# Block attention of the first two batches: pairs of heads on a block diagonal, ahead of the MLP

## The chip, the cores and the metric

The kernel runs on one core of one Trainium2 chip. The metric is device microseconds of one execution, the median of the runs. TensorE is called PE below, VectorE DVE, ScalarE ACT, GpSimd POOL; SP is the engine that issues the DMAs.

## What is computed

```python
scores = scale * np.matmul(q, k.transpose(0, 1, 3, 2))     # 8 batches, 8 heads, 576 tokens, 64 dims
scores = np.where(block_i >= block_j, scores, -1000000000.0)  # blocks of 64 tokens
scores = scores - np.max(scores, axis=-1, keepdims=True)
attn = np.exp(scores)
attn = attn / (np.sum(attn, axis=-1, keepdims=True) + 1e-09)
x = np.matmul(attn, v)                                     # heads side by side: (8, 576, 512)
u = x + (x.transpose(0, 2, 1) @ U @ V).transpose(0, 2, 1)
y = u + np.maximum(u @ w_ch1, 0.0) @ w_ch2                 # 512 -> 2048 -> 512
out = (sigmoid(causal_conv5(y, conv_w)) * (y @ w_val)) @ w_out
```

q, k and v are float32, the weights float64. A query of block i sees the keys of blocks 0 to i.

## The kernel before, in words

**Stages.** 64 heads (8 batches of 8) go through attention, the 4608 tokens through the MLP in nine groups of 512 (group 0, 1, ...), and then through the gate stage. A group of the MLP has 16 steps f. Step f computes one slice h of 128 hidden features (`emit_h1`, L833, 12 matmuls), and with a lag of one step its share of the four accumulators (`emit_o`, L885, 12 matmuls). All these products are split into a high and a low fp32r part, so each is three matmuls.

**Attention is a generator.** `attention()` yields after each piece of work. Ahead of the MLP a loop draws pieces until one yields True. After that `gap()` draws them between the matmuls of the MLP, four gaps in a step; `aim(g)` sets how many pieces a gap draws: 72 pieces over 60 gaps in group 0, 68 over 60 in the others. A group begins only when the batch that it needs is mixed; what is missing by then is drawn at once, with no MLP work between (`while g > 0 and not pace[2]`). PE runs in program order; the other engines' queues are ordered by the framework's scheduler.

**Two kinds of heads.** Heads 0 to 15 (`NQ`, two batches) work by queries. `emit_q_bank` (L404) multiplies 128 queries with their keys, with K zero outside its head's 64 rows (`kz`, the tiles za and zb). DVE writes the mask into the PSUM banks (L418 to L422), takes row maxima (L425) and scales them (L427 to L432); ACT takes the exponential out of PSUM (L440). `emit_q_turn` transposes the result on PE (L456) and ACT copies it back (L457). Heads 16 to 63 work by keys (`emit_s_piece`, L381): the two heads of a pair lie on rows 0 to 63 and 64 to 127 of the array, and DVE works out and subtracts the maxima (L474 to L512). For all heads `emit_pv` (L604) multiplies with V, whose tile `vstk` has 64 columns of ones beside the 64 of V, so that the row sums come out as rows 64 to 127; ACT copies values (L605) and sums (L606), and `emit_norm_a`, `emit_norm_b` turn the sums and scale the values (L614 to L617 and L623 on DVE, L624 on POOL). From head `FIRST_SPLIT` = 18 on, V and the exponentials are split into fp32r parts; before that they are plain fp32, which takes two matmul instructions per product.

**Order.** `tick(n)` does the scores of head n, the values of head e = n - 2 and the transposes of head e + 1. `mixing` does the products with U and V for a pair of heads (`mix_T` L664, L672; `mix_G` L680; `mix_H` L703), which gives the u tiles of the MLP. Ticks 0 to 11 run ahead of the MLP, tick 12 to half of tick 20 in group 0, up to half of tick 28 in group 1.

**Conversions.** w_ch1 and w_ch2 are converted from float64 in 32 pieces (`split_w1`, `split_w2`): a load of 512 KB into one of two `raw` buffers, ACT (L118), four DVE operations (L120, L122, L123, L141), ACT and POOL for the parts (L89, L95), and for w_ch2 a store to `w2_s`, from which `load_w2` (L821) fetches it. The loop ahead of the MLP starts one at piece C0 = 4 and at every C1 = 12 pieces after it, 7 in all; group 0 starts four at step 0 and two at each further step.

```python
    for i, done in enumerate(stream):
        if i == UVAT:
            setup_uv()
        if i >= C0 and (i - C0) % C1 == 0 and len(convs) > 2 * NF - CMAX:
            conv(1)
        if done:
            break
```

Of the kernel before, what the change touches and what calls it, by code (L numbers as in the profile page):

```python
# [17 lines left out]
P = 128  # L18
# [4 lines left out]
def attn_moe_gate_kernel(ctx: ExitStack, tc: tile.TileContext, q, k, v, U, V, w1, w2, wval, convw, wout, out):  # L23
# [21 lines left out]
    FIRST_SPLIT = 2 * H + 2  # L45
# [6 lines left out]
    C0 = 4  # L52
# [23 lines left out]
    NPART = 0  # L76
    PAT = (0,1)
    URG = True
    UVAT = 10
# [222 lines left out]
    def setup_att():  # L302
        for t in vstk:
            pool.memset(t[:, :, D:P], 1.0)
            pool.memset(t[0:D, NK - 1, :], 0.0)
        for a in range(2):
            for t in kz:
                pool.memset(t[own[1 - a], a, :], 0.0)
# [60 lines left out]
    def emit_s_piece(pn, i):  # L369
# [31 lines left out]
    eqs = {}
    qmax = {}

    def emit_q_bank(n, i):  # L404

        a = n % 2
        tq, z = qkt[n // 2]
        if i == 0:
            s0, s1 = (s_p.tile([P, w], F32, tag=f"s{h}", name=f"s{h}") for h, w in enumerate(sw))
            eqs[n] = {3: s0[:, 0:4 * P], 1: s0[:, 4 * P:6 * P], 0: s1[:, 0:P], 2: s1[:, P:4 * P], 4: rot("m" if a else "mb", 1)}  # L410
            t = tiny_p.tile([P, 2 * NTT + 2], F32, tag="rq", name="rq")
            qmax[n] = (t[:, 0:NTT + 1], t[:, NTT + 1:], psum["a"].tile([P, 512], F32, tag="a", name="pS"))
        r, nm, _ = qmax[n]
        ps = psum["a"].tile([P, 512], F32, tag="a", name="pS") if i else _
        for t, k0, k1, o in qbanks[i]:
            pe.matmul(ps[:, o:o + k1 - k0], tq[:, kslice(t)], z[:, a, k0:k1], start=True, stop=True)  # L416
        if i == 0:
            vec.memset(ps[0:D, 4 * P - D:4 * P], MASKED)  # L418
        elif i == 2:
            vec.memset(ps[0:D, 3 * P - D:3 * P], MASKED)  # L420
        elif i == 3:
            vec.memset(ps.rearrange("p (c w) -> p c w", w=D)[0:D, 1:6:4, :], MASKED)  # L422
        for t, k0, k1, o in qbanks[i]:
            c = t + (k0 > 0)
            vec.reduce_max(r[:, c:c + 1], ps[:, o:o + k1 - k0], axis=AX.X)  # L425
        if i == 0:
            x = vec.tensor_scalar(nm[:, 3:4], r[:, 3:4], -scale, None, op0=ALU.mult)  # L427
        elif i == 2:
            vec.tensor_tensor(r[:, 4:5], r[:, 4:5], r[:, 5:6], op=ALU.max)
            x = vec.tensor_scalar(nm[:, 2:5:2], r[:, 2:5:2], -scale, None, op0=ALU.mult)  # L430
        elif i == 3:
            x = vec.tensor_scalar(nm[:, 0:2], r[:, 0:2], -scale, None, op0=ALU.mult)  # L432
        if i == 1:
            eqs[n]["wait"] = ps
            return
        noted(1, x)
        noted(3, x)
        for t, k0, k1, o in qbanks[i] + (qbanks[1] if i == 2 else []):
            src = eqs[n]["wait"] if i == 2 and t == NTT - 1 and k0 == 0 else ps
            act.activation(eqs[n][t][:, k0:k1], src[:, o:o + k1 - k0], AF.Exp, bias=nm[:, t:t + 1], scale=scale)  # L440

    def emit_q_turn(n):

        eq = eqs.pop(n)
        for i, (half, c0, blocks) in enumerate(tbanks):
            if c0 == 0:
                e = e_p.tile([P, sw[half]], F32, tag=f"e{half}", name="e")
                est[n, half] = (e,)
            ps = ps_p.tile([P, 512], F32, tag="a", name="pE")
            o = c = D if i == 0 else 0  # L450
            todo = []
            for t, j in blocks:
                todo.append((t == NTT - 1, o if t < NTT - 1 else o - D, t, j))
                o += P if t < NTT - 1 else D
            for _, at, t, j in sorted(todo, key=lambda x: not x[0]):
                pe.transpose(ps[:, at:at + P], eq[t][:, kslice(j)], ident)  # L456
            act.copy(est[n, half][0][:, c0:c0 + o - c], ps[:, c:o])  # L457
# [80 lines left out]
    def emit_est(n):  # L538

        if not 0 <= n < NH:  # L540
            return
        if n < NQ:
            with tc.high_priority():
                emit_q_turn(n)
            return
# [169 lines left out]
    def tick(n, mixed, last=B * NP):  # L715
# [3 lines left out]
        new, old = n < NH, 0 <= e < NH  # L719

        load_v(e + 1)
        for i in range(4):
            if n < NQ:
                with tc.high_priority():
                    emit_q_bank(n, i)
            elif new and n % 2 == 0:
                emit_s_piece(n // 2, i)
            if i == (0 if n % 2 else 3) and new and n >= NQ:
# [3 lines left out]
        if new:  # L732
            if n >= NQ:
                emit_max_b(n)
# [3 lines left out]
        if new and n >= NQ:  # L738
# [7 lines left out]
        if new and n >= NQ:  # L746
# [26 lines left out]
    def attention():  # L773

        for n in range(H + DEPTH + MORE):
            yield from tick(n, 0, NP)
        k = 0
        for at in range(2 * (H + MORE), 4 * (NP - 1) + H0 + 1):
            while k < NPART and at - 2 * (H + MORE) >= PAT[k]:
                h1_part(k)  # L780
                k += 1
            yield from mixing(at, 0, NP)
        for n in range(H + DEPTH + MORE, NH + DEPTH + HPOS // 2):
            yield from tick(n, NP)
# [264 lines left out]
    def aim(g):  # L1049

        if not pace[2]:
            end = 4 * (2 * NP - 1) + HPOS
            count = 6 * (end // 2 - H - MORE + 1) - 2 * (end % 2 == 0)
# [109 lines left out]
```

## Time and profile before

| | us |
|---|---|
| three runs | 1476.24, 1476.52, 1479.33; median 1476.52 |
| span of the profiled execution | 1473.3 |
| ahead of the MLP (0 to the first h) | 128.5 |
| group 0 of the MLP | 180.1 |
| group 1 | 134.3 |
| groups 2 and 3 | 133.6, 133.1 |
| group 8, with no attention in it | 86.3 |

The span reaches from the first to the last instruction of the profiled execution. Stages are cut at the first h of each group (192 matmuls of L833 each). A busy PE in the profile includes the tail of each matmul, so that 85% busy may still hide small holes.

### The profile page before, as it was taken

Reading aid. Unit: us, or ns where it says so; the run is one execution under the profiler, and the core shown is the slowest. Engines: PE = TensorE matmul, PEld = TensorE weight load, DVE = VectorE, ACT = ScalarE, POOL = GpSimd, SP = SyncE. Lnnn points to the kernel's source line nnn. Section 1 sums busy time; section 2 is a strip of 40 time slices with the busy share of each in tenths; the row PEclk is TensorE's granted clock in tenths of the full one; section 3 lists DMA queues with packets and bytes.
Section 4 is the critical chain, followed back from the end, with each engine's and each line's share of the span. In section 5 each row is a group of like instructions: output and inputs, shape, how many; then the busy total and the mean of one; then the engine's idle time right before and its main releaser. Section 6 shows DMA issues by size and latency. Waiting matters only on the chain.

```text
span 1473.3 us, 20082 instructions
## 1 busy us (share of the span) xinstructions
PE 1426.3 (97%) x6706; PEld 1102.3 (75%) x6706; DVE 1054.8 (72%) x2224; ACT 718.5 (49%) x1529; POOL 297.8 (20%) x420
## 2 busy tenths in 40 slices
PE   6888899899999999999999999999999999999999
PEld 3656666677777777777777777777888888788887
DVE  7878877967786888777778878777224326399991
ACT  4676564555555546565555555555322221344332
POOL 2113332212121112112211211121122100343310
PEclk9999999999999999999999999999999999999999
DMA  6445764543343434333434433332255433223311
GB/s 123 104 106 154 217 210 130 152 110 96 84 102 110 95 96 111 96 86 82 124 82 111 114 83 96 96 95 70 86 159 167 147 128 123 92 72 101 109 56 65
DMA packets 246288, 163.56 MB, mean 111 GB/s; under 512 B 197669, under 2 KB 212261, under 8 KB 246186
## 3 DMA queue, kind: packets, MB, share of 16 engines
q1 hardware_dynamic: 246186, 162.29, 39.6%
q8 instruction: 53, 0.87, 0.3%
q14 instruction: 49, 0.40, 0.1%
HBM read 134.98 MB, written 27.26 MB: 110 GB/s over the span
## 4 chain that ended last, share of the span: by engine, by line
PE 82%; DVE 10%; DMA 3%; ACT 2%; issue 1%; SPq 1%; POOL 0%; DVEq 0%; ACTq 0%
PE acc L885 25%; PE h L833 25%; PE pPV L604 8%; PE o L999 7%; PE val L975 6%; PE pS L381 6%; DMA raw<-in_moe_w_ch_dram 1%; DVE wa L123 1%; DVE rq L425 1%; PE pG L680 1%; PE acc L878 1%; PE pS L416 1%; DVE wa L141 1%; PE pT L664 1%; DVE wa L120 1%
## 5 line engine op out<-in xcount | busy, mean ns | idle before, releaser
L885 PE MATMUL acc<-hh,w 128*128 128x512 f32 x1152 | 401.0, 402 | 0.0
L885 PEld LDWEIGHTS acc<-hh,w 128*128 128x128 f32 x1152 | 217.1, 188 | 67.6 <-issue 22.5
L833 PE MATMUL h<-uh,w1hi 128*128 128x512 f32 x576 | 238.5, 414 | 2.3 <-ACT lt L606 1.2
L833 PE MATMUL h<-uh,w1lo 128*128 128x512 f32 x576 | 226.4, 393 | 0.0
L885 PE MATMUL acc<-hl,w 128*128 128x512 f32 x576 | 225.9, 392 | 0.0
L833 PE MATMUL h<-ul,w1hi 128*128 128x512 f32 x576 | 225.7, 392 | 0.0
L862 DVE SCALAR_TENSOR_TENSOR hl<-h,hh 128x512 fp32r<-128x512 f32 x144 | 98.5, 684 | 143.2 <-ACT hh L861 142.0
L861 ACT ACTIVATE hh<-h 128x512 fp32r<-128x512 f32 x144 | 85.9, 596 | 173.9 <-PE h L833 167.9
L833 PEld LDWEIGHTS h<-uh,w1hi 128*128 128x128 f32 x576 | 108.6, 189 | 45.7 <-issue 20.4
L95 POOL TENSOR_TENSOR vlo<-vstk,vhi 128x320 fp32r<-128x320 f32 x46 | 43.0, 934 | 455.3 <-ACT vhi L89 389.2
L833 PEld LDWEIGHTS h<-uh,w1lo 128*128 128x128 f32 x576 | 108.4, 188 | 24.2
L885 PEld LDWEIGHTS acc<-hl,w 128*128 128x128 f32 x576 | 108.8, 189 | 19.8 <-issue 0.7
L833 PEld LDWEIGHTS h<-ul,w1hi 128*128 128x128 f32 x576 | 108.7, 189 | 19.6 <-issue 1.3
L957 DVE SCALAR_TENSOR_TENSOR gt<-yb,cw,gt 128x516 f32<-128x516 f32 (+1 forms) x144 | 115.2, 830 | 1.4
L381 PE MATMUL pS<-tq,tk 64*128 64x320 f32 (+4 forms) x576 | 96.7, 429 | 1.5 <-DVE hl L862 0.8
L95 POOL TENSOR_TENSOR yl<-yb,yh 128x512 fp32r<-128x512 f32 (+7 forms) x64 | 66.9, 1078 | 107.4 <-ACT yh L89 107.3
L386 ACT COPY s<-pS 128x320 f32<-128x320 f32 (+2 forms) x128 | 60.2, 497 | 48.7 <-PE pS L381 47.5
L95 POOL TENSOR_TENSOR ul<-xt,uh 128x512 fp32r<-128x512 f32 (+7 forms) x64 | 53.8, 850 | 108.0 <-ACT uh L89 107.9
L536 ACT ACTIVATE s<-s 128x448 f32<-128x448 f32 (+1 forms) x62 | 44.0, 710 | 64.8 <-DVE s L512 64.8
L381 PEld LDWEIGHTS pS<-tq,tk 64*128 64x128 f32 x576 | 43.8, 185 | 37.8 <-issue 22.2
L512 DVE TENSOR_TENSOR s<-s,mb 128x64 f32<-128x64 f32 (+4 forms) x160 | 68.7, 493 | 0.3
L605 ACT COPY xt<-pPV 64x128 f32<-64x128 f32 (+1 forms) x128 | 50.1, 391 | 25.8 <-PE pPV L604 23.9
(169 smaller groups left out, 2758.8 us busy)
## 6 DMA issues: line engine op xcount, KB each, us to landing
w<-w_s SPq DMA_DIRECT2D x144, 512.0 KB, 3.3
rawq<-in_q_dram SPq DMA_DIRECT2D x128, 72.0 KB, 2.8
rawk<-in_k_dram SPq DMA_DIRECT2D x128, 72.0 KB, 3.1
out_dram<-ot SPq DMA_DIRECT2D x35, 256.0 KB, 2.0
vstk<-in_v_dram SPq DMA_DIRECT2D x64, 128.0 KB, 2.7
raw<-in_moe_w_ch_dram SPq DMA_DIRECT2D x64, 128.0 KB, 2.8
raw<-in_moe_w_ch_dram SPq DMA_DIRECT2D x16, 512.0 KB, 3.9
w_s<-wo SPq DMA_DIRECT2D x16, 512.0 KB, 3.3
```

Source lines behind the costliest of these rows:

```text
L95: eng.tensor_tensor(o, i, f32(h), op=ALU.subtract)
L381: pe.matmul(t[:, o:o + w], tk[me, kslice(j)], tq[me, a0:a1], start=True, stop=True)
L386: act.copy(stt[n][half_of[j]][:, d:d + o], t[:, 0:o])
L512: noted(3, vec.tensor_tensor(sv(n, j), sv(n, j), mb[:, q0[j]:], op=ALU.subtract))
L604: pe.matmul(o_, l_, r_, start=(i == 0), stop=(i == len(todo) - 1))
L833: pe.matmul(ps[:, 0:n], w[:, d, fs], x[:, d, 0:n], start=(d == 0 and i == 0), stop=(d == ND - 1 and i == 2))
L861: act.activation(hh[:, 0:n], ps[:, 0:n], AF.Relu)
L862: latest[0] = vec.scalar_tensor_tensor(hl[:, 0:n], ps[:, 0:n], 0.0, f32(hh[:, 0:n]), op0=ALU.max, op1=ALU.subtract)
L885: pe.matmul(acc[d][:, 0:n], w[:, wi, ds], x[:, 0:n], start=False, stop=(f == NF - 1 and i == 2))
L957: vec.scalar_tensor_tensor(gt[d][:, 0:gw], y[:, d, j:j + gw], cw[:, d, j:j + 1], gt[d][:, 0:gw], op0=ALU.mult, op1=ALU.add)
L975: pe.matmul(ps[:, 0:n], w[:, d, es], x[:, d, 0:n], start=(i == 0), stop=(i == 3 * ND - 1))
L999: pe.matmul(ps[:m, cs], x[:, e, a:a + m], w[:, e, cs], start=(i == 0), stop=(i == 3 * ND - 1))
```

## The change

Heads 0 to 15 are taken by pairs and by blocks of 64 queries. Q of a pair goes on a block diagonal (`qdiag`: columns (block, head, query)), so that one matmul gives 64 queries of both heads against exactly the keys they may see; the mask goes. A pair is worked in two halves u, blocks 6 to 8 and blocks 0 to 5. ACT sums the exponentials as it computes them (`accum_out`), and the exponentials are divided before they are transposed: blocks 0 to 5 on DVE, 6 to 8 on POOL. The values of the two heads are two matmuls with 64 columns of V each, written side by side on partitions 0 to 63 and 64 to 127 of one bank. All 16 heads start ahead of the MLP (`slot(u)`, u = 0 to 15); slots 16 to 20 are drawn in group 0, 12 pieces, and ticks 16 and later begin in group 1. Conversions ahead of the MLP: pieces 10, 22, ..., 106, nine in all. Heads 16 and 17 are split like the later ones.

```diff
-    FIRST_SPLIT = 2 * H + 2
+    FIRST_SPLIT = 2 * H
-    C0 = 4
+    C0 = 10
+    BREAK = 2 * H - 1
+    ONVEC = (0, 1, 2, 3, 4, 5)
-    UVAT = 10
+    UVAT = 14
...
+    def vpart(n):
+        c = D if n < NQ and n // 2 % 2 else 0
+        return vstk[n % 2][:, :, c:c + D]
...
+    def qdiag(t):
+        return t.rearrange("p (i a q) -> p i a q", a=2, q=D)
...
+            for a in range(2):
+                vec.transpose(qdiag(z)[own[a], :, a, :], t["q"][own[a]].rearrange("p (i q) -> p i q", q=D))
...
+                vec.transpose(tk, t["k"])
...
+    qbanks = (
+        ([(8, 0, 4 * P, 0, 0)],
+         [(8, 4 * P, S, 0, 1), (6, 0, 7 * D, D, 2)],
+         [(7, 0, 8 * D, 0, 3)]),
+        ([(5, 0, 6 * D, 0, 0), (1, 0, 2 * D, 6 * D, 1)],
+         [(4, 0, 5 * D, 0, 2), (2, 0, 3 * D, 5 * D, 3)],
+         [(3, 0, 4 * D, 0, 4), (0, 0, D, 4 * D, 5)]),
+    )
+    tbanks = (
+        ([(0, 6, 9), (4, 8, 9)], [(1, 6, 9)], [(2, 6, 9)], [(3, 6, 9)]),
+        ([(0, 0, 4)], [(0, 4, 6), (2, 4, 6)], [(1, 2, 6)]),
+    )
...
+        for i, k0, k1, o, c in todo:
+            pe.matmul(ps[:, o:o + k1 - k0], z[:, i * P:(i + 1) * P], tk[:, k0:k1], start=True, stop=True)
+        for i, k0, k1, o, c in todo:
             vec.reduce_max(r[:, c:c + 1], ps[:, o:o + k1 - k0], axis=AX.X)
...
+            act.activation(eblk[i][:, k0:k1], src[:, o:o + k1 - k0], AF.Exp, bias=nm[:, c:c + 1], scale=scale, accum_out=l[:, c:c + 1])
+    def emit_q_norm(u):
...
+        vec.tensor_scalar(l[:, 0:n], l[:, 0:n], 1e-9, None, op0=ALU.add)
+        vec.reciprocal(rec[:, 0:n], l[:, 0:n])
...
+                    (vec if i in ONVEC else pool).tensor_scalar(eblk[i][:, 0:w], eblk[i][:, 0:w], rec[:, c:c + 1], None, op0=ALU.mult)
+    def emit_q_turn(u, b):
+        ps = (ps_p if b % 2 else psum["a"]).tile([P, 512], F32, tag="a", name="pE")
...
+                pe.transpose(ps[:, c:c + P], eblk[i][:, kslice(j)], ident)
...
+        act.copy(e, ps[:, 0:c])
+    def emit_q_pv(u, part):
...
+                for a in range(2):
+                    pe.matmul(
+                        ps[own[a], (a0 - i0) * D:(a1 - i0) * D].rearrange("p (i q) -> p i q", q=D),
+                        vpart(2 * pn + a)[:, j, :], ev[:, :, a, :],
...
+            act.copy(xt[:, i0 * D:i1 * D], turned.pop(u)[:, 0:(i1 - i0) * D])
+    def slot(u):
...
+    def attention():
+        for a in range(4):
+            load_v(a)
+        for u in range(NQ + 5):
+            for done in slot(u):
+                yield done
+            if u == BREAK:
+                yield True
+            if u == NQ + 1:
+                ones_v()
+        for n in range(NQ, NH + DEPTH + HPOS // 2):
+            yield from tick(n, 2 * NP)
...
-            count = 6 * (end // 2 - H - MORE + 1) - 2 * (end % 2 == 0)
...
+            count = 12
             pace[:] = [0.0, (count if g == 0 else 8 * H + NP) / (4.0 * NF - SPARE), 0]
```

`slot(u)` emits, in this order and each followed by a yield: bank 0 of half u; the first part of the values of half u - 2; bank 1; the second part of the values (after which, for odd u, V of the next pair is loaded); bank 2 and the division of half u (for odd u also `prep_t` of the next pair, with its loads of q and k); the transposes of half u - 1; and the mixing steps, H for u = 2 pair + 6, G at + 5, T at + 4.

## Rows read from the trace of the kernel before

**Rows 1.** The page: busy time, share of the span, instructions of each engine.

```profile
PE 1426.3 (97%) x6706; PEld 1102.3 (75%) x6706; DVE 1054.8 (72%) x2224; ACT 718.5 (49%) x1529; POOL 297.8 (20%) x420
```

**Rows 2.** Stages: us, then PE, weight loads, DVE, ACT, POOL busy, clock, DMA share.

```profile
0.00:128.50 128.50, 101.86 (x477) 67.90 (x477) 97.38 (x281) 80.77 (x194) 25.55 (x38) 0.97 0.50 114
128.50:308.60 180.10, 164.42 (x731) 118.36 (x732) 149.61 (x309) 99.22 (x211) 54.92 (x60) 0.97 0.59 172
308.60:442.90 134.30, 133.59 (x657) 102.61 (x657) 104.78 (x232) 73.53 (x156) 24.15 (x44) 1.00 0.38 98
...
1177.40:1263.70 86.30, 86.30 (x382) 71.51 (x381) 37.67 (x55) 16.95 (x29) 0.11 (x1) 1.00 0.38 122
```

**Rows 3.** PE's longest wait ahead of the MLP: us in total, times, longest.

```profile
PE pE L456 <- ACT lt L606: 7.9, 7, 2.3
```

**Rows 4.** Timeline of PE ahead of the MLP: start, us to the last end.

```profile
45.71 3.41 PE L416 MATMUL pS<-za,tq 128*128 128x512 f32 x12
...
50.51 2.98 PE L604 MATMUL pPV<-e,vstk 128*128 128x128 f32 x12
...
53.76 0.27 PE L456 MATMUL pE<-ident,m 128*128 128x128 f32 x1
53.87 0.49 PE L456 MATMUL pE<-ident,s 128*128 128x128 f32 x3
```

**Rows 5.** Timeline of PE in group 2: a pair's scores between matmuls of the MLP.

```profile
600.62 0.39 PE L833 MATMUL h<-uh,w1lo 128*128 128x512 f32 x1
600.94 0.81 PE L381 MATMUL pS<-tq,tk 64*128 64x320 f32 x4
601.67 0.50 PE L833 MATMUL h<-uh,w1hi 128*128 128x512 f32 x1
```

**Rows 6.** Groups of DVE from 7 to 128.5 us: busy us, mean ns, idle before.

```profile
L425 DVE TENSOR_REDUCE rq<-pS 128x1 f32<-128x512 f32 (+2 forms) x72 | 31.2, 469 | 0.7 <-PE pS L416 0.2
...
L614 DVE STREAM_TRANSPOSE t<-lt 128x576 f32<-128x576 f32 x5 | 3.9, 774 | 3.9 <-ACT lt L606 3.9
...
L705 DVE TENSOR_TENSOR xt<-pH,xt 128x512 f32<-128x512 f32 (+1 forms) x8 | 3.4, 436 | 0.2
L623 DVE STREAM_TRANSPOSE t<-r 128x576 f32<-128x576 f32 x4 | 3.1, 768 | 0.0
...
L422 DVE MEMSET pS<- 64x128 f32 x12 | 2.0, 165 | 1.0 <-PE pS L416 0.8
...
L430 DVE TENSOR_SCALAR rq<-rq 128x2 f32<-128x2 f32 x12 | 1.9, 156 | 0.0
```

**Rows 7.** Timelines: steps of one conversion on DVE, and POOL beside it.

```profile
145.89 0.42 DVE L120 TENSOR_SCALAR wa<-wa 128x512 f32<-128x512 f32 x1
...
146.81 1.71 DVE L123 SCALAR_TENSOR_TENSOR wa<-raw,wa 128x512 uint32<-128x512 uint32 x1
148.55 0.69 DVE L141 SCALAR_TENSOR_TENSOR wa<-raw,wa 128x512 uint32<-128x512 uint32 x1
...
146.70 1.27 POOL L95 TENSOR_TENSOR w1lo<-wa,w1hi 128x512 fp32r<-128x512 f32 x1 [2.01 <-ACT w1hi L89]
```

**Rows 8.** ACT ahead of the MLP: a copy (timeline), the exponentials (group).

```profile
51.24 0.27 ACT L605 COPY xt<-pPV 64x128 f32<-64x128 f32 x1
...
L440 ACT ACTIVATE s<-pS,rq 128x512 f32<-128x512 f32 (+3 forms) x46 | 23.0, 537 | 15.9 <-DVE rq L427 10.4 <-DVE rq L430 4.3 <-DVE rq L432 1.0
```

**Rows 9.** DMA issues from 128.5 to 275 us: count, KB, us to landing.

```profile
raw<-in_moe_w_ch_dram SPq DMA_DIRECT2D x12, 512.0 KB, 3.9
...
w<-w_s SPq DMA_DIRECT2D x11, 512.0 KB, 4.3
```

**Rows 10.** The last DVE step of each conversion (L141), first and last stretch.

```profile
128.50:150.00 21.50, 4.34 (x5) 1.00 0.61 181
...
255.00:280.00 25.00, 2.26 (x4) 1.00 0.73 200
```

**Rows 11.** PE's scores by keys (L381) in group 1.

```profile
308.60:442.90 134.30, 16.01 (x96) 7.30 (x96) 1.00 0.38 98
```

More of the change, by code (lines that the diff above doesn't have):

```diff
@@ new lines, in attn_moe_gate_kernel, with emit_q_bank @@
+    half_i = ((6, 9), (0, 6))
+    halves = {}
+    turned = {}
+    def emit_q_bank(u, b):
+        pn, g = divmod(u, 2)
+        z, tk = qkt[pn]
+        if b == 0:
+            t = tiny_p.tile([P, 24], F32, tag="rq", name="rq")
+            halves[u] = [t[:, 6 * c:6 * c + 6] for c in range(4)] + [None]
+        r, nm, l, _, wait = halves[u]
+        ps = psum["a"].tile([P, 512], F32, tag="a", name="pS")
+        todo = qbanks[g][b]
+        for i, k0, k1, o, c in todo:
+            pe.matmul(ps[:, o:o + k1 - k0], z[:, i * P:(i + 1) * P], tk[:, k0:k1], start=True, stop=True)
+        for i, k0, k1, o, c in todo:
+            vec.reduce_max(r[:, c:c + 1], ps[:, o:o + k1 - k0], axis=AX.X)
+        if g == 0 and b == 0:
+            halves[u][4] = ps
+            return
+        c0, c1 = todo[0][4], todo[-1][4] + 1
+        todo = [(ps, x) for x in todo]
+        if wait is not None:
+            vec.tensor_tensor(r[:, 0:1], r[:, 0:1], r[:, 1:2], op=ALU.max)
+            vec.tensor_copy(r[:, 1:2], r[:, 0:1])
+            c0 = 0
+            todo = [(wait, qbanks[0][0][0])] + todo
+            halves[u][4] = None
+        x = vec.tensor_scalar(nm[:, c0:c1], r[:, c0:c1], -scale, None, op0=ALU.mult)
@@ L436, in emit_q_bank @@
         noted(1, x)
         noted(3, x)
[L438 to L457, printed above, removed]
+        for src, (i, k0, k1, o, c) in todo:
+            act.activation(eblk[i][:, k0:k1], src[:, o:o + k1 - k0], AF.Exp, bias=nm[:, c:c + 1], scale=scale, accum_out=l[:, c:c + 1])
@@ new lines, in emit_q_pv @@
+    def emit_q_pv(u, part):
+        pn, g = divmod(u, 2)
+        if part == 0 and g == 0:
+            xts[pn] = x_p.tile([P, S], F32, tag="xt", name="xt")
+        xt = xts[pn]
+        i0, i1 = half_i[g]
+        if part == 0:
+            turned[u] = ps_p.tile([P, 512], F32, tag="a", name="pPV")
+        ps = turned[u]
+        n = len(tbanks[g])
+        for b in range(n)[(0, 2)[part]:(2, n)[part]]:
+            c = 0
+            e = turned.pop((u, b))
+            for k, (j, a0, a1) in enumerate(tbanks[g][b]):
+                w = (a1 - a0) * P
+                ev = e[:, c:c + w].rearrange("p (i a q) -> p i a q", a=2, q=D)
+                c += w
+                last_ = b == n - 1 and k == len(tbanks[g][b]) - 1
+                for a in range(2):
+                    pe.matmul(
+                        ps[own[a], (a0 - i0) * D:(a1 - i0) * D].rearrange("p (i q) -> p i q", q=D),
+                        vpart(2 * pn + a)[:, j, :],
+                        ev[:, :, a, :],
+                        start=b == 0 and k == 0,
+                        stop=last_,
+                    )
+        if part == 1:
+            act.copy(xt[:, i0 * D:i1 * D], turned.pop(u)[:, 0:(i1 - i0) * D])
+            last[0] = (own[0], xt[own[0]][0:1, i0 * D:i0 * D + 1])
@@ L538, in emit_est @@
     def emit_est(n):
[L540 to L544, printed above, removed]
+        if not NQ <= n < NH:
             return
@@ L732, in tick @@
         if new:
-            if n >= NQ:
-                emit_max_b(n)
+            emit_max_b(n)
             if n % 2 == 1:
@@ L737, in tick @@
         yield from mixing(2 * e, mixed, last)
-        if new and n >= NQ:
+        if new:
             for _ in emit_max_c(n):
@@ L745, in tick @@
             yield
-        if new and n >= NQ:
+        if new:
             emit_exp(n)
@@ L1051, in aim @@
         if not pace[2]:
-            end = 4 * (2 * NP - 1) + HPOS
-            count = 6 * (end // 2 - H - MORE + 1) - 2 * (end % 2 == 0)
-            for delay, steps in ((HPOS, 2), (GPOS, 1), (TPOS, 2)):
-                count += steps * sum(2 * H <= 4 * pn + delay <= end for pn in range(NP, 2 * NP))
+            count = 12
             pace[:] = [0.0, (count if g == 0 else 8 * H + NP) / (4.0 * NF - SPARE), 0]
```

178 lines of the change are left out of this document (103 added, 75 removed).

## The prediction

> **What bounds the kernel now.** I began with the page: PE is busy 97% of the span, the next engine 72% [rows 1], so time can only come from PE's work or from holes in it. An average over stages says little here, so the second view was the busy time by stage [rows 2]. The reader is to see three things. Ahead of the MLP, PE has 101.9 us of 128.5 and DVE 97.4: neither is full, they wait for each other. Group 0 takes 180.1 us, though a group without attention takes 86.3; DVE is at 149.6 there, with most of the conversions on it. In group 1 PE is full (133.6 of 134.3) and DVE is at 78%. From group 2 on the change touches nothing: the same ticks end at the same place. So the sum is over three stages, which end at 442.9 us today, and the 1030.4 us behind them stay. The third view was what PE waits for ahead of the MLP: most of all, 7.9 us, for the copies of the row sums (L606) [rows 3]. The fourth was the timeline, for what one piece costs PE [rows 4, 5].
>
> **PE's work.** One head's scores are 1856 columns in 3.41 us [rows 4]; without some 0.25 us by which a last matmul outlasts its turn, 1.70 ns a column. A pair takes 2 x 1856 columns now, then 64 x (1 + ... + 9) = 2880: 832 x 1.70 = 1.4 us less, 11 us over 8 pairs. Transposes go from 30 to 25 a pair at 0.11 us ((0.49 - 0.27) / 2, from three in a row and one alone [rows 4]): 40 x 0.11 = 4.4 us less. The values keep their columns, 3200 a pair, 2.73 us a head (2.98 less the tail [rows 4]). Their cost is open, since the trace shows no two matmuls side by side in columns of the array. The nearest row has two side by side in rows: four scores of 320 columns on 64 rows each end after 0.81 us [rows 5], where one after the other they would take 4 x 0.27 + 0.25 = 1.33. So at best the 43.7 us of 16 heads halve, 22 us less; at worst nothing is gained. Going in and out costs something in the same rows: L381 begins 0.32 us after a matmul of the MLP, whose turn is 0.23 (86.3 us for 382 [rows 2]), and the next one 0.73 after L381 instead of 0.54: 0.28 us a visit. The values are visited 32 times: 9 us. I take the halved time less the visits, 13 us. The Trainium skill (TensorEngine Tiling (Array Packing), Key Properties) says that a change of tiling mode, not of the tile alone, drains the engine, which speaks against many short visits; the 0.28 us agrees with it.
>
> **Ahead of the MLP.** Today this stage has 12 heads' scores and 10 heads' values, then 16 and 14. PE will need 8 x 2880 columns x 1.70 = 39 us, transposes of 15 halves 21, values of 14 heads 38 (19 + 8 with overlap), mixing some 9: 96 to 107 us, against 88 by the same prices today. DVE decides. By rows 6: maxima 80 instead of 72 in 1.03 times the columns, +2; transposes of q and k for two more pairs, at 0.77 each, +4; masks gone (2.0 in L422, as much in its two smaller siblings), -4; small steps (maxima scaled, sums added, reciprocals) 96 instead of 48 at 0.16, +8; division of blocks 0 to 5, 48 instructions of 224 columns in the mean, 0.27 each between 0.156 for two columns and 0.42 for 512 [rows 6, 7], +13; row sums no longer turned, -7 in L614 and L623, -1.5 in the steps between; mixing of one and a half pairs more (L705 has 3.4 us for four, its siblings as much), +2.6; two conversions more at 2.2 (two steps of 0.42, two of 0.69 [rows 7]), +4.5. That is +21.6. The divisions of blocks 6 to 8 go to POOL, 24 of 448 to 576 columns, nearest row 1.27 us for 512 [rows 7], and beside that row DVE's L123 took 1.71 instead of 0.69. Between nothing and 24 x 1.0 us falls on DVE; I take 5, since most of DVE's work in those moments is maxima, read from PSUM. The Trainium skill (GPSIMD Engine Reference, Specifications) says that POOL shares its SBUF interfaces with DVE and contends with some of DVE's forms; L123 agrees. If that held for each of the 24, the stage would be 19 us of DVE longer than with my 5.
>
> DVE thus goes from 97.4 to 124. Without 7 us of start, in which it has 2.3, it now works 95.1 of 121.5 us; the 7.9 us for L606 go with the sums [rows 3], which makes 84%. (124 - 2.3) / 0.84 + 7 = **152**. At 92% it would be 139, at today's 78% 163. ACT loses the eight copies of values and sums a pair for two. Its sums within the exponential have no row: between nothing and one small copy of 0.27 us [rows 8], for 88 of them 24 us; I take 0.1 each, and all of it is hidden as long as ACT is 81 of 128.5 us busy [rows 2]. The division lies between a half's last exponential and its transposes: some 6 us (maximum 0.5, exponential 0.5, four small steps, three on POOL at 1.3 [rows 6 to 8]), covered by the next half's banks and another's values, 5 to 7 us of PE; without that cover it is rival (c). SP issues the loads of q, k (16) and V (8) of four more heads in this stage; DMA is half idle there. The memsets of the ones move behind slot 17, to an idle POOL.
>
> **Group 0.** 86.3 us for the MLP and what is left of the pairs: transposes of half 15 (1.3), values of two halves (4), mixing of two to three pairs (5): 97. Conversions are 23 now, with less to hide them. A `raw` buffer goes round in 3.9 us of load [rows 9], 2.2 on DVE [rows 7] and about 1.7 for ACT and the hand-offs: 7.8 us with two buffers, 3.9 a conversion. The last w_ch1 piece is ready 22 x 3.9 + 3 = 89 us after the start and wanted at 15/16 of 97, 91; the last w_ch2 piece after 90 + 3 and a store and a load of about 4 each [rows 9], 101, and wanted at 99. SP issues in order, and the fetches of w_ch2 stand behind loads that wait for a buffer. I add 8: **105**, between 97 and 125.
>
> **Group 1.** It takes over three pairs of scores (16.0 / 4 = 4.0 us each [rows 11]) and two heads' values (2.7 each): 134.3 + 17.4 = 152. Ticks 16 to 28 are 92 pieces, and 62 gaps draw 62 x 68/60 = 70 of them. The other 22 run without the MLP: PE has 22/68 of 48 us (134.3 - 86.3), 15.5, DVE up to 22/68 of 104.8, 34 [rows 2]. Between 0 and 18 us of holes; I take 4, as DVE's part can mostly run on into group 2, where it has room: **156**. Heads 16 and 17 in split form cost much the same.
>
> **Sum.** 152 + 105 + 156 = 413 instead of 442.9, 29.9 us less: against the profiled execution's span of 1473.3 that is 1443.4. The median stands 3.2 us above that span; with them **1446.6**.
>
> **Rivals.** (a) *It goes better*: DVE at 92%, two values at a time, conversions keep up: 139 + 98 + 152 = 389, 54 less, 1422.6. For it: rows 5. Against: DVE has never been so full ahead of the MLP. 16%. The Trainium skill (TensorE: Matmul & The Clock Gate, Part 3) gives column tiles that run concurrently; no row here shows them. (b) *The values don't overlap*, so that one point of the change fails: PE has 107 + 9 = 116 us ahead of the MLP; at today's 88 of 121.5 that takes 160, from 7 us on 167; 428 in all, 15 less, 1461.6. Against it: rows 5. 12%. (c) *The chain bounds*: a half costs what a head costs today, 121.5 / 12 = 10.1 us, because maximum, exponential, sum, division and transposes follow one another; 7 + 162 = 169; 430 in all, 13 less, 1463.6. For it: both engines wait today. Against: the longest wait goes. 11%. (d) *Slower, because the conversions bound group 0.* Today 25 of them end between 128.5 and 280 us, 6.1 us each [rows 10]. At that pace 23 take 140, with store and load 148: 152 + 148 + 156 = 456, 13 more, 1489.6. It decides from 5.5 us a conversion ((442.9 - 152 - 156 - 8) / 23). For it: two buffers and SP's order stay. Against: DVE is rid of the attention that came between their steps. 13%.
>
> **How the numbers follow.** My forecast has 48%. Its own range is 1430 to 1462, from stages of 139 to 163, 97 to 115 and 152 to 160 that don't all end on one side. A measurement here can tell some 0.2%, 3 us, from no change. Faster: 48 + 16 + 12 and half of (c), 82%; same, edges of (c) and (d), 5%; slower 13%. The range reaches from 1420, inside (a), to 1478, short of (d).
>
> **What would show it.** The first h near 152 us, group 1's near 257, group 2's near 413. Right: matmuls of the values in twos, no wait of PE for sums, DVE some 84% busy ahead of the MLP, conversions 4 us apart in group 0. Wrong: values at 2.7 us a head (b), PE waiting for POOL ahead of the transposes (c), PE waiting for w1lo or w in group 0 (d), a long hole at the end of group 1.

## The result, and the profile after

The changed kernel took 1485.93 us, median of 5 runs (1485.39 to 1489.71), beside 1476.52 for the kernel before on the same chip: 1.0074 times as long, with a 95% interval of 1.0052 to 1.0097. Slower by 0.7%; 1446.6 had been predicted, in a range that ended at 1478. The profiled execution took 1485.87 us, with a span of 1484.0.

First the page, to be read beside [rows 1]: PE has 21 us less to do, ACT 16 less, DVE as much as before.

```profile
PE 1405.5 (95%) x6736; PEld 1087.3 (73%) x6736; DVE 1054.6 (71%) x2215; ACT 702.2 (47%) x1545; POOL 329.3 (22%) x442
```

Then the stages, cut at the first h of each group as in [rows 2], with the same columns. The last line is the stage ahead of the MLP without its first 7 us.

```profile
0.00:162.20 162.20, 113.03 (x670) 73.78 (x670) 122.36 (x346) 89.42 (x276) 63.77 (x64) 0.94 0.47 107
162.20:279.90 117.70, 105.28 (x470) 81.06 (x468) 86.03 (x128) 47.85 (x92) 38.90 (x33) 0.97 0.67 223
279.90:452.90 173.00, 160.84 (x761) 118.97 (x760) 143.81 (x332) 98.87 (x208) 32.09 (x65) 0.96 0.36 88
452.90:586.10 133.20, 133.20 (x658) 102.56 (x657) 106.28 (x240) 73.99 (x156) 24.17 (x45) 1.00 0.40 99
...
7.00:162.20 155.20, 113.03 (x670) 73.78 (x670) 120.31 (x344) 87.94 (x274) 59.49 (x45) 0.93 0.47 107
```

Nearly the whole difference lies in the three stages, as the prediction had it: they end at 452.9 instead of 442.9, and behind them are 1031.1 us instead of 1030.4. Two sums over them say what happened. PE's busy time fell from 399.9 us [rows 2] to 379.2 (113.0 + 105.3 + 160.8): the 21 us that the change takes from PE did go. Its idle time rose from 43.0 to 73.8, 31 us. DVE's work is the same (351.8 [rows 2], now 352.2) and lies elsewhere: 25 us more ahead of the MLP, 39 more in group 1, 64 less in group 0, where it is now idle for 32 us of 118. By stages, PE stands idle 22 us more ahead of the MLP and 11 more in group 1, and 3 less in group 0.

**Ahead of the MLP.** What PE waits for, in place of the row sums of [rows 3]: the division on POOL, then the exponentials. The 8.1 us are the start, the first loads and transposes.

```profile
PE pS L445 <- DVE tq L378: 8.1, 1, 8.1
...
PE pE L500 <- POOL s L479: 22.0, 13, 6.0
PE pE L500 <- ACT s L463: 7.7, 5, 3.2
```

The groups of this stage that answer to [rows 6 to 8] (busy us, mean ns, idle time before): maxima, divisions on DVE and on POOL, and a line that the source does not show, since each exponential with `accum_out` is followed by a separate read of the accumulator.

```profile
L447 DVE TENSOR_REDUCE rq<-pS 128x1 f32<-128x512 f32 (+4 forms) x80 | 33.0, 449 | 11.4 <-PE pS L445 11.0
L479 DVE TENSOR_SCALAR s<-s,rq 128x384 f32<-128x384 f32 (+5 forms) x48 | 18.5, 454 | 0.2
...
L479 POOL TENSOR_SCALAR s<-s,rq 128x576 f32<-128x576 f32 (+2 forms) x24 | 38.9, 1634 | 61.3 <-DVE rq L474 31.7 <-ACT t L503 24.7 <-ACT x L91 4.9
...
L463 ACT ACTIVATION_READ_ACCUMULATOR s<-pS,rq 128x1 f32 x80 | 16.5, 206 | 0.0
```

The timeline of one half's end (start, us, what; in brackets the idle time before) shows the chain in one piece: the last exponential, the read of its sum, the reciprocal, three divisions in a row of 1.74 us each, and PE, which has nothing else to do meanwhile. From 60.10 to the twelve transposes at 66.53 are 6.4 us, in which PE stood idle for 3.5 and 1.3.

```profile
59.58 0.64 ACT L463 ACTIVATE s<-pS,rq 128x448 f32<-128x448 f32 x1
...
60.10 0.21 ACT L463 ACTIVATION_READ_ACCUMULATOR s<-pS,rq 128x1 f32 x1
...
60.88 0.18 DVE L474 RECIPROCAL rq<-rq 128x4 f32<-128x4 f32 x1
...
61.26 5.21 POOL L479 TENSOR_SCALAR s<-s,rq 128x576 f32<-128x576 f32 x3 [2.48 <-DVE rq L474]
...
64.78 0.48 PE L500 MATMUL pE<-ident,s 128*128 128x128 f32 x1 [3.48 <-POOL s L479]
...
66.53 2.82 PE L500 MATMUL pE<-ident,s 128*128 128x128 f32 x12 [1.28 <-POOL s L479]
```

**Group 0.** PE's waits there are for `hl`, a step of the MLP on DVE, which stands in DVE's queue behind steps of the conversions; and ACT waits for the loads of the conversions.

```profile
PE acc L998 <- DVE hl L975: 8.1, 7, 2.2
PE acc L998 <- ACT hh L974: 2.1, 2, 1.4
...
ACT wa L120 <- DMA raw<-in_moe_w_ch_dram: 33.0, 18, 3.3
```

**Group 1.** PE is busy for 160.8 us of the 173.0 here, 27 us more than in [rows 2], and idle for 12.2. The scores (first line, L406) take 33.4 us where [rows 11] has 16.0, the values (second line, L719) 28.2.

```profile
279.90:452.90 173.00, 33.40 (x168) 15.97 (x168) 0.96 0.36 88
...
279.90:452.90 173.00, 28.23 (x150) 24.79 (x150) 0.96 0.36 88
```

The values of this stage in the kernel before (L604) took 21.4:

```profile
308.60:442.90 134.30, 21.36 (x120) 18.76 (x120) 1.00 0.38 98
```

The last h of the group ends at 412 us, and from 420 to 448 PE has no matmul of the MLP at all: attention and mixing are drawn alone, with waits for DVE and for ACT's copies of the scores.

```profile
PE pG L795 <- DVE x L97: 5.3, 2, 5.2
PE pS L406 <- ACT za L411: 2.7, 2, 2.1
```

In the last 23 us of the stage DVE is 97% busy (22.3 of 23), and PE's granted clock is 0.83 and 0.61 of full speed in the mean: after that wait of 5.2 us, part of the time passes at the lower of its two levels (1.2 instead of 2.4 GHz).

```profile
430.00:440.00 10.00, 6.91 (x36) 5.50 (x36) 9.65 (x26) 3.34 (x9) 1.78 (x2) 0.83 0.16 31
440.00:453.00 13.00, 10.37 (x23) 6.17 (x24) 12.68 (x30) 8.86 (x18) 3.25 (x8) 0.61 0.18 46
```

### The profile page after: what moved, and what is told of

Its sections match the earlier page's. It is cut to its first block, busy times and chain, and to the rows that moved or that the text cites. A ratio compares the mean times of both kernels' runs of the same rounds, so it can differ in the third digit from the quotient of the medians.

```text
span 1484.0 us, 20191 instructions
## 1 busy us (share of the span) xinstructions
PE 1405.5 (95%) x6736; PEld 1087.3 (73%) x6736; DVE 1054.6 (71%) x2215; ACT 702.2 (47%) x1545; POOL 329.3 (22%) x442
## 4 chain that ended last, share of the span: by engine, by line
PE 77%; DVE 8%; DMA 4%; ACT 2%; issue 1%; POOL 1%; SPq 0%; ACTq 0%; DVEq 0%; POOLq 0%
PE acc L998 24%; PE h L946 23%; PE pPV L719 7%; PE o L1112 7%; PE val L1088 6%; PE pS L406 5%; DMA raw<-in_moe_w_ch_dram 3%; DVE wa L125 1%; PE pG L795 1%; DMA y_s<-y 1%; PE acc L991 1%; DVE wa L143 1%; ACT wa L120 1%; PE pT L779 1%; DVE m L595 1%
## 5 line engine op out<-in xcount | busy, mean ns | idle before, releaser
L946 PE MATMUL h<-uh,w1hi 128*128 128x512 f32 x576 | 234.2, 407 | 0.0
L406 PE MATMUL pS<-tq,tk 64*128 64x320 f32 (+4 forms) x576 | 100.2, 432 | 5.7 <-ACT za L411 4.0
L411 ACT COPY s<-pS 128x320 f32<-128x320 f32 (+2 forms) x128 | 59.9, 497 | 45.8 <-PE pS L406 42.6
L406 PEld LDWEIGHTS pS<-tq,tk 64*128 64x128 f32 x576 | 46.3, 187 | 42.9 <-issue 21.3
L655 ACT ACTIVATE s<-s 128x448 f32<-128x448 f32 x64 | 45.2, 711 | 53.5 <-DVE s L631 53.3
L500 PE MATMUL pE<-ident,s 128*128 128x128 f32 x200 | 32.3, 307 | 31.6 <-POOL s L479 22.0
```

The source lines that it names most:

```text
L406: pe.matmul(t[:, o:o + w], tk[me, kslice(j)], tq[me, a0:a1], start=True, stop=True)
L411: act.copy(stt[n][half_of[j]][:, d:d + o], t[:, 0:o])
L946: pe.matmul(ps[:, 0:n], w[:, d, fs], x[:, d, 0:n], start=(d == 0 and i == 0), stop=(d == ND - 1 and i == 2))
```

## The experiments

All edits are against the changed kernel unless another is named. Times of stages are from each kernel's one profiled execution, medians and ratios from its timed runs against the kernel before on the same chip.

| kernel | ahead of MLP | group 0 | group 1 | end | median | ratio (95%) |
|---|---|---|---|---|---|---|
| before | 128.5 | 180.1 | 134.3 | 442.9 | 1476.52 | |
| after | 162.2 | 117.7 | 173.0 | 452.9 | 1485.93 | 1.0074 (1.0052 to 1.0097) |
| e1_dve_div | 151.9 | 120.7 | 171.6 | 444.2 | 1483.69 | 1.0057 (1.0035 to 1.0079) |
| e2_pace_g1 | 159.8 | 117.6 | 169.1 | 446.5 | 1483.03 | 1.0050 (1.0032 to 1.0068) |
| e3_ticks_back | 160.5 | 144.2 | 134.8 | 439.5 | 1473.48 | 0.9984 (0.9973 to 0.9995) |
| e4_one_head | 161.6 | 118.9 | 172.6 | 453.1 | 1485.53 | 1.0069 (1.0051 to 1.0087) |
| e5_ticks_dve | 152.4 | 142.5 | 134.7 | 429.6 | 1462.17 | 0.9907 (0.9892 to 0.9922) |
| e6_ticks_div8 | 153.9 | 146.4 | 134.2 | 434.5 | 1465.79 | 0.9933 (0.9918 to 0.9948) |
| e7_no_sum | 151.1 | 120.1 | 171.7 | 442.9 | 1475.25 | 0.9991 (0.9979 to 1.0003) |
| e8_conv_early | 184.7 | 118.3 | 173.1 | 476.1 | 1508.69 | 1.0213 (1.0189 to 1.0236) |
| e9_serial_v | 151.0 | 142.4 | 135.3 | 428.7 | 1460.91 | 0.9896 (0.9866 to 0.9926) |
| e10_no_div | 129.4 | 125.8 | 170.4 | 425.6 | 1457.21 | 0.9867 (0.9831 to 0.9903) |
| e11_conv_free | 160.9 | 110.5 | 173.4 | 444.8 | 1479.32 | 1.0025 (1.0008 to 1.0041) |
| e12_ticks_dve_c24 | 140.1 | 162.1 | 134.8 | 437.0 | 1467.45 | 0.9939 (0.9921 to 0.9957) |

### e1: all divisions on DVE

```diff
-    ONVEC = (0, 1, 2, 3, 4, 5)
+    ONVEC = (0, 1, 2, 3, 4, 5, 6, 7, 8)
```

> Edit: the division of blocks 6 to 8 goes from POOL to DVE as well. Theory H (holes: the new kernel lost its gain in three separate places, the first being PE waiting 22 us ahead of the MLP for POOL's divisions of 1.6 us each): DVE gets 24 more operations of about 0.4 us, 10 us, the waits go, the first h comes at 145 to 153 us instead of 162.2, the median at 1470 to 1477. Rival D (DVE is the bound in all three stages, PE's waits are only where that shows): the 10 us are added to DVE's 122 of 162, the first h comes at 162 to 172, the median at 1486 to 1496.

In the trace the stage ahead of the MLP is 10.3 us shorter, though DVE has 18 divisions more in it. PE now waits for DVE in the same place:

```profile
PE pE L500 <- DVE s L479: 15.6, 5, 4.7
...
PE pE L500 <- DVE rq L459: 6.8, 2, 3.8
```

```profile
7.00:151.90 144.90, 117.31 (x669) 78.84 (x670) 119.24 (x360) 89.23 (x277) 20.88 (x20) 0.90 0.49 112
```

DVE's work is 119.2 us where it was 120.3: what POOL took off it (a net 18 divisions in this window) had been paid back by slower steps beside POOL, some 6 us. DVE's share is 82% instead of 77.5%. The stage came as theory H had it; the median lies between the two theories and does not settle it: the profiled execution was the quickest of the four (1477.19, the others 1483.0 to 1484.6), and the interval overlaps that of the kernel after. The same edit on e3 does (e5).

### e2: more pieces a gap in group 1

```diff
-            pace[:] = [0.0, (count if g == 0 else 8 * H + NP) / (4.0 * NF - SPARE), 0]
+            pace[:] = [0.0, (count if g == 0 else 92 if g == 1 else 8 * H + NP) / (4.0 * NF - SPARE), 0]
```

> Edit: group 1 draws its 92 pieces of attention evenly over its gaps (92/60 a gap instead of 68/60), so that none is left for the end. Theory H: the run of 22 pieces without the MLP cost 39 us for 15.5 us of PE's work, and that hole closes; group 1 takes 153 to 160 us instead of 173, the median is 1466 to 1473. Rival D: DVE had 144 us busy in group 1 and PE will now wait for it between the matmuls of the MLP; group 1 stays at 168 to 175, the median at 1481 to 1488.

Group 1 is 169.1 us instead of 173.0, as rival D had it, with no stretch without the MLP at its end and the clock back at 0.99. So the hole at the end was not the loss, only the place where it showed. PE now has 158.0 us of work in the stage and DVE 147.7; where PE is not full, as in 20 us of its middle (second line), DVE is.

```profile
277.40:446.50 169.10, 158.01 (x761) 117.40 (x760) 147.71 (x335) 98.10 (x208) 33.62 (x66) 0.99 0.37 90
...
320.00:340.00 20.00, 16.96 (x85) 12.71 (x83) 19.55 (x42) 13.17 (x27) 4.80 (x9) 1.00 0.39 91
```

PE's waits (10.6 us) are nearly all for ACT's copies of the scores (L411), though ACT is busy for 98 us of 169. One of them, with what ACT had waited for:

```profile
326.39 1.35 ACT L411 COPY s<-pS 128x512 f32<-128x512 f32 x3 [1.80 <-DVE el L97]
...
327.03 1.57 PE L406 MATMUL pS<-tq,tk 64*128 64x448 f32 x6 [0.84 <-ACT s L411]
```

That DVE stands behind these waits is read from the trace; no run takes work off DVE alone in group 1.

### e3: the later heads' first ticks back in group 0

Ticks 16 to 19 and the scores of tick 20 are drawn in group 0 again, as before the change; the pairs of heads 0 to 15 stay ahead of the MLP. The edit also leaves heads 16 and 17 unsplit again, as they were.

```diff
-    FIRST_SPLIT = 2 * H
+    FIRST_SPLIT = 2 * H + 2
...
-                yield u >= NQ and step is mix_H2 and pn == 2 * NP - 1
+                yield False
...
-            yield from tick(n, 2 * NP)
+            for k, done in enumerate(tick(n, 2 * NP)):
+                yield done or (n == NQ + 4 and k == 3)
...
-            count = 12
+            count = 36
```

> Edit: ticks 16 to 19 and the scores of tick 20 go back from group 1 into group 0, as before the change (heads 16 and 17 unsplit again, as the tiles of the split open only later in group 0). Theory H: group 1 comes back to 133 to 137 us from 173; group 0, which has 48 us of attention work less than before the change, takes 17 us of PE's work more, 134 to 145 instead of 117.7; the median 1462 to 1474. Rival D: DVE has the conversions in group 0 and gets 30 us more; group 0 goes to 150 or more and the median to 1478 to 1490.

Group 1 is back at 134.8 us, 38.2 less; group 0 takes 26.5 more. The difference, 11.7, and 1.7 ahead of the MLP make 13.4; the median fell by 12.5.

```profile
160.50:304.70 144.20, 126.52 (x565) 92.42 (x564) 121.30 (x227) 69.23 (x135) 45.77 (x52) 0.95 0.65 193
304.70:439.50 134.80, 133.61 (x658) 102.63 (x657) 105.26 (x235) 73.82 (x157) 24.57 (x45) 1.00 0.39 101
```

DVE's columns (the third busy time) show the move: 143.8 us of work in group 1 became 105.3, and group 0, where DVE had had 86.0, holds 121.3 without being full. Nearly the same work costs 38 us in group 1 and 26 in group 0. Both of PE's parts shrink: of the 11.7 us, 6.0 are its busy time over the two groups (266.1 to 260.1; the two heads left unsplit are in it), 5.7 its idle time (24.6 to 18.9).

### e4: the values one head after the other

```diff
-            for k, (j, a0, a1) in enumerate(tbanks[g][b]):
...
-                for a in range(2):
+            for a in range(2):
+                c = 0
+                for k, (j, a0, a1) in enumerate(tbanks[g][b]):
```

> Edit: the values of a pair are emitted head after head instead of in turns, so that no two matmuls in different columns of the array stand next to each other. Theory H: the two run at the same time now, and apart they need 19 us more of PE ahead of the MLP, of which a part falls into the waits for POOL: the first h at 168 to 180 us instead of 162.2, the median 1492 to 1504. Rival D, or if being side by side is not what made them cheap: first h within 3 us of 162, the median 1483 to 1489.

Nothing moved, and nothing follows from it, since the edit hardly does what it was meant to: it parts the heads within a bank only, and five of a pair's seven banks hold a single block of keys, where the order stays as it was. In the trace the two heads' matmuls still run side by side, and the values took PE 27.6 us instead of 26.4. e9 parts them by place.

### e5: e1 and e3 together

> Edit: ticks 16 to 19 and the scores of tick 20 back in group 0, and all divisions on DVE. Theory H2 (ahead of the MLP the division on POOL holds the transposes, in group 1 DVE is full, in group 0 it has room): the two gains add; first h at 150 to 154 us, group 0 143 to 147, group 1 134 to 136, median 1462 to 1469. Rival G (the 10 us that the division alone gained in the profile are lost again in most runs, whose median gained 2): median 1470 to 1476.

Both gains add up: 1462.17 us, 0.9907 of the kernel before (0.9892 to 0.9922), 1.6% less than the kernel after, faster than both. Beside e3 the stage ahead of the MLP is 8.1 us shorter and the median 11.3 us less: here the division on POOL shows in the medians.

### e6: e5 with block 8's division on POOL

```diff
-    ONVEC = (0, 1, 2, 3, 4, 5, 6, 7, 8)
+    ONVEC = (0, 1, 2, 3, 4, 5, 6, 7)
```

> Edit: as the kernel with both, but the division of block 8 stays on POOL, beside DVE's blocks 6 and 7. Theory H2: three in a row on POOL were what held the transposes; one of 1.8 us beside two of 0.5 on DVE costs PE's wait nothing more and saves DVE 4 us: first h at 146 to 152, median 1458 to 1468. Rival S (POOL's operation stretches DVE's steps next to it, as it did in the conversions): first h at 152 to 157, median 1465 to 1475.

One division of three on POOL still costs something, as rival S had it: 1465.79, 3.6 us more than e5. In the profiled executions 1.5 us lie ahead of the MLP and 3.9 in group 0, which has no such division, so that part is not explained. This split of the work is no better than DVE alone.

### e7: no sums in the exponential

```diff
-            act.activation(eblk[i][:, k0:k1], src[:, o:o + k1 - k0], AF.Exp, bias=nm[:, c:c + 1], scale=scale, accum_out=l[:, c:c + 1])
+            act.activation(eblk[i][:, k0:k1], src[:, o:o + k1 - k0], AF.Exp, bias=nm[:, c:c + 1], scale=scale)
```

> Edit: the exponentials of heads 0 to 15 take no sums; the sums are set to 1, so the division by the row sum is left out (its instructions stay). The trace of the changed kernel has 80 reads of the accumulator on ACT of 0.206 us, 16.5 us in all. Theory H2: they are hidden, since POOL and DVE hold the chain: first h at 159 to 163 us, median 1482 to 1487. Rival A (they lie in the chain from maximum to transpose, ten a pair): first h at 150 to 156, median 1473 to 1479.

The 80 reads of the accumulator, 16.5 us of ACT, are gone, and the stage is 11.1 us shorter, the median 10.7 less. ACT was 55% busy in it, so its work as such was hidden; the sums as a link of the chain were not. The edit takes out more than the reads, though: with constant sums DVE's additions and reciprocals no longer wait for the exponentials. In the kernel after, DVE stood idle for 11.4 us ahead of these two steps, in e7 for 0.3:

```profile
L473 DVE TENSOR_SCALAR rq<-rq 128x4 f32<-128x4 f32 (+1 forms) x16 | 4.8, 298 | 6.8 <-ACT s L463 6.7
...
L471 DVE TENSOR_TENSOR rq<-rq 128x1 f32<-128x1 f32 x8 | 1.3, 159 | 4.6 <-ACT s L463 4.5
```

How much of the 11 us is the reads and how much these waits, no run tells apart. PE's wait for POOL halves, though POOL does the same divisions:

```profile
PE pE L501 <- POOL s L480: 11.0, 4, 4.2
```

### e8: eight more conversions ahead of the MLP

```diff
-    C1 = 12
+    C1 = 6
```

> Edit: a conversion at every 6 pieces instead of 12 ahead of the MLP, 17 instead of 9, so 8 fewer in group 0. Theory H2: group 0 is held by its conversions on DVE (the low parts of h wait for DVE 8 us) and falls to 98 to 106 us from 117.7; ahead of the MLP DVE is the fuller engine, each conversion costs 2.2 us at 78%, 8 of them 20 to 25, first h at 180 to 188; median 1490 to 1498. Rival E (ahead of the MLP the halves' chain is the bound and DVE has room in it): first h at 164 to 172, median 1474 to 1482.

Each of the eight costs 2.8 us there (22.5 / 8), and group 0 is not shorter with 16 conversions instead of 24. So in this kernel the number of conversions does not set group 0, neither theory's median came, and the prediction's rival (d) is not what happened. It is the largest loss of the study, 2.1% over the kernel before.

### e9: e5, with the values of a pair not side by side

Both heads' values are written to partitions 0 to 63, of two banks; ACT copies twice as often.

```diff
-            turned[u] = ps_p.tile([P, 512], F32, tag="a", name="pPV")
+            turned[u] = [ps_p.tile([P, 512], F32, tag="a", name="pPV") for _ in own]
...
-                        ps[own[a], (a0 - i0) * D:(a1 - i0) * D].rearrange("p (i q) -> p i q", q=D),
+                        pss[a][own[0], (a0 - i0) * D:(a1 - i0) * D].rearrange("p (i q) -> p i q", q=D),
```

> Edit, on the kernel with ticks and division moved (first h at 152.4 us, median 1462.2): the values of both heads go to partitions 0 to 63, of two banks, so that the two matmuls use the same columns of the array and can't run at once; ACT copies them out in four copies a pair instead of two. Theory H2: the trace shows the two 6 to 7 ns apart, 252 of them in 26 us ahead of the MLP; one after the other they need some 19 us more of PE, of which a good part falls into PE's waits for DVE: first h at 158 to 172, median 1470 to 1484. Rival: DVE alone bounds that stage, PE's time is free: first h at 151 to 156, median 1461 to 1467.

The values now cost PE 44.4 us ahead of the MLP instead of 25.3 in e5 (first fence: e9; second: e5; PE busy, weight loads).

```profile
0.00:151.00 151.00, 44.37 (x252) 29.02 (x252) 0.97 0.49 110
```

```profile
0.00:152.40 152.40, 25.32 (x252) 14.01 (x252) 0.89 0.50 112
```

The overlap is real, and here it is worth nothing, as the rival had it: the stage takes 151.0 us instead of 152.4, the kernel 1460.91 instead of 1462.17 (ratios 0.9896 and 0.9907, their intervals overlap). Two things make up for it. PE waits less, 9 us for DVE ahead of the transposes (first fence, e9) where e5 has 22 (second). And all its other work takes 83.7 us in e9 and 93.0 in e5, at a granted clock of 0.97 and 0.89, so that its whole busy time differs by 9.8 us and not by 19.

```profile
PE pE L500 <- DVE s L479: 5.5, 3, 4.1
PE pE L500 <- DVE rq L459: 3.3, 1, 3.3
```

```profile
PE pE L500 <- DVE s L479: 15.3, 5, 4.3
...
PE pE L500 <- DVE rq L459: 6.8, 2, 3.8
```

The same shape in the two kernels' timelines, eight matmuls of 192 columns, in the kernel after and in e9:

```profile
73.12 0.87 PE L526 MATMUL pPV<-e,vstk 128*64 128x192 f32 x8
```

```profile
64.30 1.51 PE L526 MATMUL pPV<-e,vstk 128*64 128x192 f32 x8
```

The Trainium skill (TensorE: Matmul & The Clock Gate, Part 3) says that tiles in different column groups run concurrently; the 0.87 beside 1.51 us agrees.

### e10: no division

```diff
-                    w = D * (i + 1)
-                    (vec if i in ONVEC else pool).tensor_scalar(eblk[i][:, 0:w], eblk[i][:, 0:w], rec[:, c:c + 1], None, op0=ALU.mult)
+                    pass
```

> Edit, on the changed kernel: the division is left out, on POOL (39 us busy) and on DVE (22 us); the exponentials are transposed as they are. Theory H2: maxima, sums and division are one chain from bank to transposes; without its last part PE's 22 us of waits for POOL and DVE's 22 us go: first h at 130 to 142 us instead of 162.2, the rest as it was, median 1454 to 1468. Rival (another wait, of the exponentials on ACT or of the maxima, ends as late): first h at 148 to 160, median 1472 to 1485.

The stage takes 129.4 us, 32.8 less, while DVE has 22 us less to do behind the start (120.3 to 98.2, 18.5 of them the division). At the share of 77.5% that DVE had, 22 us of work are 28 of the 33, so this run alone does not part DVE's work from the division's place in the chain; e5 beside e3 does, with DVE's work alike.

```profile
7.00:129.40 122.40, 105.91 (x669) 69.73 (x670) 98.17 (x293) 86.62 (x272) 20.20 (x20) 0.97 0.58 126
```

Of PE's 22.0 us of waiting for POOL and 7.7 for ACT ahead of the transposes mainly this is left:

```profile
PE pE L499 <- ACT s L463: 3.4, 3, 1.5
```

### e11: conversions in group 0 without their DVE steps

```diff
+            if where[0] == CV1:
+                act.activation(a, f32(raw[:, :, 1]), AF.Abs)
...
```

> Edit, on the changed kernel: the conversions that run in group 0 keep their loads, ACT's and POOL's parts and the stores, but leave out their four DVE steps, so the weights are wrong. Theory K (in group 0 PE is late because hl waits in DVE's queue behind conversion steps, whatever their number): group 0 falls from 117.7 us to 98 to 104, median 1466 to 1474. Rival L (the loads, stores and fetches through SP and the raw buffers hold it): 110 to 118, median 1478 to 1487.

Group 0 takes 110.5 us instead of 117.7. Theory K's 98 to 104 did not come; time and median lie at the low end of rival L's ranges. DVE's work in it falls from 86.0 to 20.6, and the waits for `hl` go, 8.1 us to 0.2; others stay or come:

```profile
PE acc L1001 <- DMA w<-w_s: 4.6, 1, 4.6
PE acc L1001 <- ACT hh L977: 2.3, 1, 2.3
...
PE acc L1001 <- DVE hl L978: 0.2, 1, 0.2
```

So the conversions' steps on DVE cost 7 us of group 0, and with them go the waits for `hl`, which stands behind them in DVE's queue. The rest of the 13 us by which group 0 is above the predicted 105 has another cause.

### e12: e5 with four conversions fewer ahead of the MLP

```diff
-    C1 = 12
+    C1 = 24
```

> Edit, on the kernel with ticks and division moved: a conversion only at every 24 pieces ahead of the MLP, 5 instead of 9, so 4 more in group 0. With 17 of them group 0 did not get shorter and each one ahead of the MLP cost 2.8 us. Theory H2: first h at 139 to 144 us instead of 152.4, group 0, which now has 17 us more of PE's work than the conversions need at 4.3 us each, stays at 142 to 148; median 1449 to 1457. Rival M (four more in group 0 at 4.3 us lengthen it): group 0 at 155 to 162, median 1462 to 1470.

The stage ahead is 12.3 us shorter, group 0 19.6 longer, 1467.45 in all, 5.3 more than e5. With the ticks in group 0, four more conversions there cost 4.9 us each (rival M), against 3.1 ahead of the MLP. PE now waits for the weights themselves, which come late, among others:

```profile
PE acc L999 <- DMA w<-w_s: 5.1, 1, 5.1
...
PE h L947 <- ACT w1hi L91: 3.7, 2, 3.3
```

Beside e8: a conversion cost some 3 us ahead of the MLP in both kernels, and in group 0 nothing or 5.

## Why the prediction was wrong

It was 40 us too low by stages: 162.2 against 152, 117.7 against 105, 173.0 against 156. PE's savings, on which its argument began, were of the right order (28 us by its terms, 21 of busy time gone). Ahead of the MLP PE waited for a chain; in groups 0 and 1 its own work came out 8 to 9 us above the price, and it waited 12 us in each.

**Ahead of the MLP, +10.** The step that failed is the 84% in "(124 - 2.3) / 0.84 + 7 = 152". DVE's work was priced right: 120.3 us behind the start, 121.7 predicted. The price of POOL beside DVE was too (5 taken, some 6 by e1). But the share was taken to rise because one wait of PE went, and it stayed at 77.5%, "today's 78%", for which the prediction's own bound was 163; it measured 162.2. The new chain took the place of the old wait, and its terms were each sized too small: divisions of 1.27 us on POOL were 1.63, the sums' 0.1, of which "all of it is hidden", were 0.206 and a link that was not hidden (e7: 11 us, with DVE's waits for them), and the cover of "5 to 7 us of PE" for the division was not there: PE waited 22 us for it. Rival (c) was the mechanism, and near in size: 155.2 / 16 = 9.7 us a half where it said 10.1. It had been given 11%, because "the longest wait goes"; what comes in its place had not been followed to its end. With the division on DVE (e1) the share was 82% and the stage 151.9: the predicted 152, by another kernel.

**The values side by side.** As PE time their price held: 27 us ahead of the MLP (19 + 8), 26.4 measured. Apart they cost more than the 38 it had (44.4 in e9), so the overlap saves 19 us there and not 11. As time nothing came back. Rival (b) put 15 us on it (428 instead of 413); without the overlap, the stage of e9 was 1.4 us shorter than that of e5.

**Group 0, +13.** The conversions were counted nearly right (24, between 162.2 and 265.5, 4.3 us each; 23 at 3.9 predicted), and neither rival (d)'s pace nor their number decided (e8). "I add 8" stands beside 12.4 us of idle time, with another cause: not weights that come late, but for 8.1 us `hl` behind conversion steps in DVE's queue; without these steps the stage is 7 us shorter (e11); "DVE is rid of the attention" was right and did not help, since the queue's order is what PE waited for. The term that failed most is the 97: PE was busy 105.3 us. What makes up those 8 is not settled, since fewer conversions (e8) leave them as they are; the clock of 0.97 is 3.5 of them at most (0.03 x 117.7).

**Group 1, +17.** Two terms failed, about half each. The first is PE's "134.3 + 17.4 = 152": PE was busy 160.8 us. Three pairs' scores at 4.0 us each added 17.4 us instead of 12 (5.8 a pair; 17.7 in e2 at a clock of 0.99), two heads' values 6.9 instead of 5.4. Why a pair's scores cost more here than in [rows 11] is open. The second is "Between 0 and 18 us of holes; I take 4": 12.2 came. The 152 adds work to PE alone, though DVE's part of the three pairs had a price in [rows 2]: (104.8 - 37.7) / 4 = 16.8 a pair, 50 for three, 155 in all. So the same rows named DVE as a second engine near full; 143.8 came, 147.7 with the pace of e2, and neither engine was kept busy: 169 even with the MLP spread over all of it. "DVE's part can mostly run on into group 2" was wrong as well: group 2 begins only when its own batch is mixed, so the work has to end in group 1.

What is shown: the division's place in the chain (e5 beside e3), the sums as a link of it (e7), that the loss in group 1 goes with the pieces drawn there and not with the hole at its end (e2, e3), and that the overlap of the values brings no time ahead of the MLP (e9 beside e5). What stays open is part of group 0, DVE's share in the loss of group 1, which is read from traces alone, and why e1's runs spread over 7 us.

## What to carry to other kernels

When a change moves work from one stage to another, add it up for every engine of the stage that receives it, not only for the one that is full today, and take its price there with some doubt: three pairs' scores cost 17 us where the rows said 12. A chain through four engines is priced by its length from end to end against the work that can cover it, and a small link in it costs time however idle its engine is: the sums cost 11 us with ACT 55% busy. Before work is taken off an engine, see whether that engine waits in that stage: here 19 us of TensorE were worth nothing, lost to other waits and to a lower clock, while moving 24 divisions to another engine and 24 pieces to another stage turned 0.7% slower into 0.9% faster.

## What the runs showed of the hardware

An exponential that also sums is two instructions on ACT: the ACTIVATE, and a read of its accumulator of 0.206 us, 80 of them here.

A multiplication by one number a row took POOL 1.634 us in the mean for 448 to 576 columns, more than [rows 7]'s 1.27 for a subtraction of two tiles of 512; on DVE the same three blocks took 0.65, 0.48 and 0.45 in e1. The Trainium skill (GPSIMD Engine Reference, opening) calls DVE roughly twice as fast for elementwise work; here the factor is about three, and these rows decide.

Ahead of the MLP the granted clock was 0.89 in e5, with PE busy 118 of 152 us, and 0.97 in e9, with PE busy 128 of 151: the kernel with more work for PE had the higher clock and ended no later. Both are means of stretches at either of its two levels, 1.2 and 2.4 GHz. The busy share alone does not order them: the kernel after had 0.94 with PE busy 113 of 162 us.
